# An attention and feed-forward kernel: phi, k and v on 128 partitions, and a front ordered by a list scheduler in the source

## The chip, the cores and the metric

The kernel runs on one core of a Trainium2 chip. TensorE (PE, with its weight loads PEld), VectorE (DVE), ScalarE (ACT), GpSimd (POOL) and SyncE (SP) each take their own instructions strictly in order; they wait for each other by semaphores. SP issues all loads of the front. The metric is the device time of one execution in microseconds (us), the median of several runs.

## What is computed

Four sequences b with eight heads of 576 positions each (head size 64, 32 memory slots). Attention goes through the memory; then come two feed-forward layers over all 2304 positions.

```python
a = softmax(phi, over slots)              # phi: (4, 8, 576, 32); the maximum is taken over positions
k_m = einsum('bhsm,bhsd->bhmd', a, k)     # v_m alike from v
attn = softmax(q @ k_m.T / 8)             # 32 columns
x = (attn @ v_m) as (2304, 512)
x = silu(x @ w_in) @ w_out                # 512 -> 2048 -> 512
out = ((x @ w_a) * (x @ w_b)) @ w_out2    # 512 -> 1536 -> 512
```

In the reference `phi - np.max(phi, axis=2)` takes the maximum over the 576 positions, for each slot. The weights come as 64-bit floats and are turned on the chip into two fp32r tiles each, a high (h) and a low part (l); each product is three fp32r matmuls (hh, hl, lh).

## The kernel before

The kernel has a front (attention of four sequences, and the first quarter f = 0 of the first layer for some units), the rest of the first layer, and the second layer. The front is what changes.

For each sequence b the front does the following. `weights(b)` (L443) takes the maximum of phi over positions on DVE (L450, tile mxa), across partitions by a PE transpose (mxt, L455) and a second maximum (mx, L459), brings it back to all partitions with a matmul (bc, L465), subtracts it (L472) and exponentiates (L475, tile ph). `memory(b)` (L493) multiplies ph by k and v (tile kvp, L506; one group of matmuls for each half hg of the heads, and one against a column of ones for the sums), normalises (rec, kvn), and makes kmT, the diagonal kbd (L548) and, over vt (L526), the value tiles vbd_hi and vbd_lo. `turn_q` (L535) transposes q into qT, `scores` (L542) makes sc by PE and x by a DVE transpose, and `softmax_part` (L566) makes x into at_hi and at_lo: maximum mxq, subtraction, Exp, sum smq, reciprocal, product, transpose xt, split. `vw_first` (L245) multiplies vbd by the weights w_in (tile mp, then m0h, m0l for b = 0, m1h, m1l for b = 1 and so on), so that a unit of the feed-forward layer is hp = m x at (`emit_h`, L279), silu, g, and yp = w_out x g (`emit_y`, L303).

phi, k and v lie on 96 partitions with 6 positions each (L416, L424), q on 128. The eight weight tiles of f = 0 go through `load_w` (L93): a 512 KB load into one of three buffers st, then e and t on ACT and DVE, with L124 or L122 the last to read st, and a split into h and l.

The source calls these pieces in an order written out by hand (L593 to L670); on each engine the framework's scheduler then orders the instructions. A load whose buffer is still read waits on SP, and all loads behind it wait too. The feed-forward units from the second half of b = 2 on follow in loops (L685). Weight tiles of f = 1 are loaded at fixed steps of the units (`due`, L331).

## Time and profile before

| | |
|---|---|
| median of 3 runs | 905.0 us (903.12 to 907.53) |
| profiled execution | 902.69 us |
| its span, first to last instruction | 900.9 us |
| PE busy in the span | 844.9 us (94%) |
| DVE, ACT, POOL busy | 536.2, 406.4, 162.5 us |
| mean granted TensorE clock | 0.962 of full speed |

In the page's forty slices PE is below 9 tenths in the first four (5, 3, 5, 8) and in the last one only (4), and the granted clock is below full in the first four and the last as well. A slice is 22.5 us long. So the time in which PE does not work at full speed lies in the first 90 us and in the last 20.

### The profile page before, as it was taken

What the parts mean: (1) busy time and instruction counts of PE and PEld (TensorE: products, weight loads), DVE (VectorE), ACT (ScalarE), POOL (GpSimd) and SP (SyncE); (2) the same over time, 40 slices, a digit from 0 to 9 for tenths busy, and PEclk for the clock granted to TensorE, in tenths of its full rate; (3) what the DMA queues carried; (4) which work ended last, traced back from release to release, by engine and by line L of the source; (5) the groups of instructions that cost most, each with busy time, mean ns of one, the idle gap of its engine ahead of it and who ended that gap; (6) DMA issues with size and microseconds to landing.
All of it is one profiled execution on the core that took longest, in us unless ns stands there. A gap on an engine that the chain in (4) does not pass through costs nothing.

```text
span 900.9 us, 14125 instructions
## 1 busy us (share of the span) xinstructions
PE 844.9 (94%) x5654; PEld 798.6 (89%) x5654; DVE 536.2 (60%) x980; ACT 406.4 (45%) x819; POOL 162.5 (18%) x160
## 2 busy tenths in 40 slices
PE   5358999999999999999999999999999999999994
PEld 4247989889999999999999999999999999999993
DVE  3699787887677676766665555545555453332221
ACT  2347676686565566655443333333333342222110
POOL 3454014422110211211221111101111110000000
PEclk7577999999999999999999999999999999999997
DMA  9988410356652554554764434424333330111101
GB/s 211 238 203 209 107 28 25 106 129 132 150 106 48 129 109 103 114 110 109 173 140 94 94 65 89 117 51 102 85 68 83 70 59 1 36 36 36 34 22 51
DMA packets 48858, 87.16 MB, mean 97 GB/s; under 512 B 3480, under 2 KB 24984, under 8 KB 48792
## 3 DMA queue, kind: packets, MB, share of 16 engines
q1 hardware_dynamic: 32664, 56.89, 23.7%
q0 software_dynamic: 16128, 29.37, 18.5%
q8 instruction: 44, 0.72, 0.3%
q14 instruction: 22, 0.18, 0.1%
HBM read 52.17 MB, written 4.72 MB: 63 GB/s over the span
## 4 chain that ended last, share of the span: by engine, by line
PE 83%; DVE 6%; DMA 5%; issue 2%; SPq 1%; ACT 1%; POOL 0%; DVEq 0%; POOLq 0%; ACTq 0%
PE ab L742 33%; PE yp L312 20%; PE op L763 17%; PE hp L288 9%; DMA st<-in_moe_w_in_dram 3%; PE mp L268 1%; PE mp L256 1%; PE sc L556 1%; DVE t L113 1%; DMA kv<-in_v_dram 1%; DMA wo_1l<-t_wo 1%; DVE qT L539 1%; SPq L427 1%; SPq L98 0%; DVE gl L300 0%
## 5 line engine op out<-in xcount | busy, mean ns | idle before, releaser
L747 DVE TENSOR_TENSOR asb<-ab,asb 128x384 f32<-128x384 f32 x72 | 40.1, 557 | 200.9 <-PE ab L742 200.9
L746 ACT ACTIVATE asb<-ab 128x384 f32<-128x384 f32 x72 | 35.4, 491 | 152.0 <-PE ab L742 145.4
L79 ACT ACTIVATE ph<-asb 128x384 fp32r<-128x384 f32 x72 | 37.5, 521 | 119.0 <-DVE asb L747 119.0
L298 ACT ACTIVATE g<-hp 128x288 f32<-128x288 f32 x128 | 52.2, 411 | 80.1 <-PE hp L288 71.9
L300 DVE TENSOR_TENSOR gl<-g,gh 128x288 fp32r<-128x288 f32 x128 | 62.2, 488 | 38.7 <-ACT gh L299 38.3
L187 POOL DMA_DIRECT2D t_w<-e_w x36 | 31.9, 885 | 145.8 <-DVE e_w L183 126.1
L318 DVE TENSOR_TENSOR y<-yp,y 128x288 f32<-128x288 f32 x104 | 47.3, 456 | 18.2 <-PE yp L312 17.5
L299 ACT ACTIVATE gh<-g 128x288 fp32r<-128x288 f32 x128 | 56.4, 444 | 3.6 <-PE yp L312 0.3
L75 DVE TENSOR_TENSOR pl<-asb,ph 128x384 fp32r<-128x384 f32 x72 | 39.9, 555 | 20.7 <-ACT ph L79 20.7
L79 ACT ACTIVATE yh<-y 128x768 fp32r<-128x768 f32 (+1 forms) x48 | 29.5, 676 | 25.5 <-PE ab L742 25.5
L312 PE MATMUL yp<-gh,wo_1l 128*128 128x288 f32 x128 | 37.8, 295 | 1.6 <-DMA wo_1l<-t_wo 1.6
L312 PE MATMUL yp<-gh,wo_0h 128*128 128x288 f32 x128 | 38.4, 300 | 0.1
L312 PE MATMUL yp<-gh,wo_2h 128*128 128x288 f32 x128 | 38.2, 298 | 0.0
L312 PE MATMUL yp<-gl,wo_3h 128*128 128x288 f32 x128 | 37.8, 297 | 0.0
L312 PE MATMUL yp<-gl,wo_2h 128*128 128x288 f32 x128 | 37.8, 295 | 0.0
L312 PE MATMUL yp<-gl,wo_0h 128*128 128x288 f32 x128 | 37.8, 295 | 0.0
L312 PE MATMUL yp<-gh,wo_2l 128*128 128x288 f32 x128 | 37.8, 295 | 0.0
L312 PE MATMUL yp<-gl,wo_1h 128*128 128x288 f32 x128 | 37.7, 296 | 0.0
L312 PE MATMUL yp<-gh,wo_3h 128*128 128x288 f32 x128 | 37.7, 295 | 0.0
L312 PE MATMUL yp<-gh,wo_1h 128*128 128x288 f32 x128 | 37.7, 294 | 0.0
L312 PE MATMUL yp<-gh,wo_0l 128*128 128x288 f32 x128 | 37.7, 294 | 0.0
L312 PE MATMUL yp<-gh,wo_3l 128*128 128x288 f32 x128 | 37.6, 294 | 0.0
(416 smaller groups left out, 2857.5 us busy)
## 6 DMA issues: line engine op xcount, KB each, us to landing
t_w<-e_w POOLq DMA_DIRECT2D x36, 256.0 KB, 4.7
st_wi<-in_moe_w_in_dram SPq DMA_DIRECT2D x12, 512.0 KB
st_wo<-in_moe_w_out_dram SPq DMA_DIRECT2D x12, 512.0 KB
st_w<-in_moe_w_a_dram SPq DMA_DIRECT2D x12, 512.0 KB
st_w<-in_moe_w_b_dram SPq DMA_DIRECT2D x12, 512.0 KB
st_w<-in_moe_w_out_dram SPq DMA_DIRECT2D x12, 512.0 KB
kv<-in_k_dram SPq DMA_DIRECT2D x8, 576.0 KB
kv<-in_v_dram SPq DMA_DIRECT2D x8, 576.0 KB
```

The lines of the kernel that those rows point to most:

```text
L75: eng_lo.tensor_tensor(out=lo, in0=src, in1=hi.bitcast(F32), op=ALU.subtract)
L79: nc.scalar.activation(out=out, in_=in_, func=AF.Copy)
L288: nc.tensor.matmul(hp, a[:, cs], x[b][:, kc, ts], start=(n == 0), stop=(n == 5))
L298: nc.scalar.activation(out=g32, in_=hp, func=AF.Silu)
L299: nc.scalar.activation(out=gh, in_=g32, func=AF.Copy)
L300: nc.vector.tensor_tensor(out=gl, in0=g32, in1=gh.bitcast(F32), op=ALU.subtract)
L312: nc.tensor.matmul(yp, a[:, os], x, start=(n == 0), stop=(n == 3 * len(cs) - 1))
L318: nc.vector.tensor_tensor(out=ys, in0=yp, in1=ys, op=ALU.add)
L742: nc.tensor.matmul(abp, a[:, ks], yy[:, kc], start=(n == 0), stop=(n == 11))
L746: nc.scalar.activation(out=asb, in_=ps[0], func=AF.Copy)
L747: nc.vector.tensor_tensor(out=asb, in0=ps[1], in1=asb, op=ALU.mult)
L763: nc.tensor.matmul(o_t[x], a[:, xs], w, start=(c == 0 and n == 0), stop=(c == 3 and n == 2))
```

## The change

phi, k and v are laid on 128 partitions: two heads side by side, 64 partitions with 9 positions each. The maximum of phi is a tree of four DVE instructions over tiles m4 and mxa instead of one reduction; its subtraction is on DVE for every b; the matmuls of kvp have 64 rows and there are 36 instead of 24 in a group. The softmax of the scores is done in two halves for every b. The front is no longer written in order: each piece is a generator that announces, before every instruction or group, its engine and a length in ns; `run` takes the one that can start first, by these lengths and by rank, and emits it. Each instruction is pinned (`Pinned`), so the framework keeps the source's order on every engine until `pinned[0] = False`, which stands behind the seventh unit. In a profile of it all pinned instructions bear one line, that of the helper.

```diff
     EPS = 1e-9
-    LATER = (nc.vector, nc.gpsimd, nc.gpsimd)
-    SPLIT = (0, 3)
-    SPLIT_W = (0,)
-    SPLIT_Q = ()
-    SUMS = (3,)
-    WARM = (16, 2, 0)
+    pinned = [True]
+
+    class Pinned:
+
+
+        def __init__(self, eng):
+            self.eng = eng
+
+        def __getattr__(self, name):
+            f = getattr(self.eng, name)
+
+            def call(*a, **k):
+                ins = f(*a, **k)
+                return tc.keep_in_program_order(ins) if pinned[0] else ins
+
+            return call
+
+    V, A, GP, T, Y = (Pinned(e) for e in (nc.vector, nc.scalar, nc.gpsimd, nc.tensor, nc.sync))
+    WARM = 16
...
-    P = 96
-    JP = S // P
+    JP = S // 64
...
-        ph = p_in.tile([P, H, JP, NM], F32, tag="ph", name="ph")
-        src = phi[b].rearrange("h (p c) m -> p h (c m)", p=P)
...
-        kv = p_in.tile([P, 2, 4, JP * D], F32, tag="kv", name="kv")
-        for i, s in enumerate((k, v)):
-            nc.sync.dma_start(
-                out=kv[:, i], in_=s[b, 4 * hg : 4 * hg + 4].rearrange("h (p c) d -> p h (c d)", p=P)
-            )
...
+    rings = dict(st=(3, []), e=(2, []), t=(2, []), ph=(2, []), kv=(2, []), qq=(3, []), qT=(1, []), x=(2, []),
+                 kvn=(1, []), mxq=(2, []), smq=(2, []), bank=(2, []), sc=(2, []), hp=(2, []), yp=(2, []), g=(8, []), m=(4, []), g32=(2, []))
...
+    def run(while_any):
+        while any(t[0] in while_any for t in tasks):
+            starts = [(start_of(t), t) for t in tasks]
+            starts = [(a, t) for a, t in starts if a is not None]
+            assert starts, [t[2] for t in tasks]
+            first, t = min(starts, key=lambda x: x[0])
+            eng = t[2][0]
+            rank, at, t = min(((t[0], a, t) for a, t in starts if t[2][0] == eng and a <= first + 200.0), key=lambda x: x[:2])
+            _, ns, _, done, takes, free, wait = t[2]
+            end = at + ns
...
+    def weights(b):
+
+        yield op("V", 1500, [f"phi{b}"])
...
-            nc.vector.tensor_reduce(
-                out=mxa, in_=e[:, hs].rearrange("p h c m -> p h m c"), op=ALU.max, axis=AX.X
-            )
...
+        m4 = p_s.tile([128, 4, 4, NM], F32, tag="m4", name="m4")
+        mxa = p_s.tile([128, 4, NM], F32, tag="mxa", bufs=2, name="mxa")
+        for o, x, y in (
+            (m4, e[:, :, 0:4], e[:, :, 4:8]), (m4[:, :, 0:2], m4[:, :, 0:2], m4[:, :, 2:4]),
+            (m4[:, :, 0], m4[:, :, 0], m4[:, :, 1]), (mxa, m4[:, :, 0], e[:, :, 8]),
+        ):
+            V.tensor_tensor(out=o, in0=x, in1=y, op=ALU.max)
...
+        yield op("V", 1350, free=[f"bc{b}"])
+        V.tensor_tensor(out=e, in0=e, in1=bc.unsqueeze(2).to_broadcast([128, 4, JP, NM]), op=ALU.subtract)
+        yield op("A", 1150, done=f"w{b}")
+        A.activation(out=e, in_=e, func=AF.Exp)
...
+            yield op("T", 3000, [f"w{b}", f"kv{b}{hg}"], take=("bank", f"kvp{b}") if hg == 0 else None,
+                     free=[f"kv{b}{hg}"] + [f"ph{b}"] * hg)
...
+                        o = slice(32 * h, 32 * h + 32)
+                        x, r = (h // 2 + b) % 2, slice(64 * (h % 2), 64 * (h % 2) + 64)
+                        T.matmul(
+                            kvp[o, hg, 2 * D :] if sums else kvp[o, hg, : 2 * D],
+                            e[r, 2 * hg + x, c],
+                            ones[r, :1] if sums else kv[r, :, x, c * D : c * D + D],
...
+            yield op("T", 1000, [f"kbd{b}"], done=f"sc{b}{hg}{hf}", take=("sc", f"sc{b}{hg}{hf}"), free=[f"qT{b}{hg}"] * hf)
...
+        sub, mul, low = HELP[b]
+        yield op("V" if sub is V else "G", 620 if sub is V else 1200, free=[f"mxq{b}{hg}"])
         sub.tensor_tensor(out=x, in0=x, in1=mx.unsqueeze(2).to_broadcast(full), op=ALU.subtract)
-        nc.scalar.activation(out=x, in_=x, func=AF.Exp, scale=scale)
-        sm = p_s.tile([128, n], F32, tag="smq", name="smq")
...
+        yield op("V", 700, free=[f"st_{name}"])
+        V.scalar_tensor_tensor(out=e, in0=low, scalar=2.0**-52, in1=e, op0=ALU.mult, op1=ALU.mult)
...
+            elif kind == "kv":
+                yield op("D", 3800, done=f"kv{b}{hg}", take=("kv", f"kv{b}{hg}"))
+                kv = st[b]["kv", hg] = p_in.tile([128, 2, 2, JP * D], F32, tag="kv", name="kv")
+                for i, s in enumerate((k, v)):
+                    src = s[b, 4 * hg : 4 * hg + 4].rearrange("(x r) (p c) d -> (r p) x (c d)", r=2, p=64)
+                    Y.dma_start(out=kv[:, i], in_=src)
...
-    load_phi(0)
+    LOADS = (
+        "phi00 wi00 kv00 q00 wi01 kv01 q01 wo00 phi10 phi20 wo01 wi02 wi03 kv10 q10 kv11 wo02 q11 kv20 q20 kv21 wo03 q21 phi30 kv30 q30 kv31 q31"
+    ).split()
+    HELP = ((GP, V, GP), (GP, GP, GP), (GP, V, GP), (GP, GP, GP))
     fill()
...
-    softmax(0, 0, nc.gpsimd, nc.gpsimd, nc.gpsimd)
-    load_kv(1, 1)
-    for kc in range(2):
-        vw_first(0, kc, (0,))
...
+    add(0, loads())
+    add(6, feed_forward())
+    for b in range(B):
+        add(2 + b, weights(b))
+        add(2 + b, memory(b))
+        add(2 + b, values(b))
+        for hg in range(2):
+            add(2 + b, scores(b, hg))
...
+    for c in range(4):
+        add((2, 2, 4, 4)[c], tile_of("wi", c, *((GP, GP), (GP, GP), (V, GP), (GP, V))[c]))
+        add((3, 2, 4, 3)[c], tile_of("wo", c, *((V, GP), (V, GP), (V, V), (V, GP))[c]))
+    run((0, 1, 2, 3, 4, 5))
+    run((1, 6))
+    pinned[0] = False
```

Three places in the order of instructions follow. In rows of before a line number tells the code; in rows of the change all have L69.

**SP, loads of the front.** st_ is the buffer of a weight tile, kv that of k or v for half of the heads of one sequence, qq that of q, ph of phi. In brackets stand the semaphores that a row waits for: DMAHW for an earlier load, the others for an engine. Before, from the fourth weight tile on (then k and v of b = 1, first half):

```order
L98 DMA st_386<-in_moe_w_out_dram 128x512 [waits DMAHW6_49,DVE_49,Activation_49]
L427 DMA kv<-in_k_dram 96x4x384 [waits DMAHW7_49,PE_49]
L427 DMA kv<-in_v_dram 96x4x384 [waits DMAHW0_49]
L98 DMA st_417<-in_moe_w_in_dram 128x2x256 [waits DMAHW1_49,Activation_49,Pool_49]
L421 DMA ph<-in_phi_dram 96x8x192 [waits DMAHW2_49,PE_49]
L427 DMA kv<-in_k_dram 96x4x384 [waits DMAHW3_49]
L427 DMA kv<-in_v_dram 96x4x384 [waits DMAHW4_49]
L98 DMA st_602<-in_moe_w_out_dram 128x512 [waits DMAHW5_49,Pool_49]
L98 DMA st_677<-in_moe_w_in_dram 128x2x256 [waits DMAHW6_49,DVE_49,Activation_49]
```

With the change, the rows from the second phi load's successor on; the second wi row here is the fourth tile of w_in, and k, v and q of b = 1 stand behind it:

```order
L69 DMA st_wo_367<-in_moe_w_out_dram 128x512 [waits DMAHW4_49,DVE_49]
L69 DMA st_wi_390<-in_moe_w_in_dram 128x2x256 [waits DMAHW5_49,DVE_49,Activation_49]
L69 DMA st_wi_502<-in_moe_w_in_dram 128x2x256 [waits DMAHW4_49,DMAHW6_49,DVE_49,Activation_49]
L69 DMA kv<-in_k_dram 128x2x576 [waits DMAHW7_49]
L69 DMA kv<-in_v_dram 128x2x576 [waits DMAHW0_49]
L69 DMA qq<-in_q_dram 64x1152 [waits DMAHW1_49]
L69 DMA qq<-in_q_dram 64x1152 [waits DMAHW2_49]
L69 DMA kv<-in_k_dram 128x2x576 [waits DMAHW3_49]
L69 DMA kv<-in_v_dram 128x2x576
```

Before, k and v of b = 1 stood behind one weight tile whose buffer was that of the first tile; they now stand behind three weight tiles, the last of which reuses the buffer of the tile that the next rows on DVE finish (st_wo_340).

**DVE, the tile of weights whose buffer is awaited.** Before, the load of the fourth w_in tile (st_677) waited for the buffer st_386, which the row with st_386 reads last:

```order
L113 SCALAR_TENSOR_TENSOR t_389<-e_388,t_389 128x512
L75 TENSOR_TENSOR vbd_lo_74<-vt,vbd_hi_72 64x2x32
L459 TENSOR_REDUCE mx<-mxt 128x2
L117 TENSOR_SCALAR e_388<-t_389 128x512
L75 TENSOR_TENSOR vbd_lo_74<-vt,vbd_hi_72 64x2x32
L124 SCALAR_TENSOR_TENSOR e_388<-st_386,e_388 128x512
L75 TENSOR_TENSOR vbd_lo_74<-vt,vbd_hi_72 64x2x32
L127 TENSOR_TENSOR t_389<-t_389,e_388 128x512
```

With the change the buffer st_wo_340 is read last by the row that has its name; the smq, x and xt above it are the softmax of b = 0, second half, and ph is the subtraction of b = 1:

```order
L69 TENSOR_REDUCE smq<-x 128x18
L69 TENSOR_SCALAR smq<-smq 128x18
L69 RECIPROCAL smq<-smq 128x18
L69 TENSOR_TENSOR x<-x,smq 128x576
L69 STREAM_TRANSPOSE xt<-x 128x576
L69 TENSOR_TENSOR ph<-ph,bc 128x1152
L69 TENSOR_SCALAR t_wo_476<-e_wo_382 128x512
L69 SCALAR_TENSOR_TENSOR t_wo_476<-e_wo_382,t_wo_476 128x512
L69 TENSOR_SCALAR e_wo_382<-t_wo_476 128x512
L69 SCALAR_TENSOR_TENSOR e_wo_382<-st_wo_340,e_wo_382 128x512
```

The last read of that buffer moved behind the whole softmax of b = 0.

**PE, scores of b = 1.** Before, the two groups of kvp for b = 1, then the scores sc of b = 1, first half, without anything of b = 2 between:

```order
L506 MATMUL kvp<-ones,ph 32x1 x24
L506 MATMUL kvp<-kv,ph 32x128 x24
L506 MATMUL kvp<-ones,ph 32x1 x24
L506 MATMUL kvp<-kv,ph 32x128 x24
L526 MATMUL vt<-ident,kvn 128x128 x2
L455 MATMUL mxt<-ident,mxa 128x96 x2
L288 MATMUL hp<-at_hi_64,m0h 128x288 x2
L556 MATMUL sc<-qT,kbd 128x288 x4
L465 MATMUL bc<-dg,ones 96x256
```

With the change, between the sc of one half of b = 1 stand the kvp groups of b = 2:

```order
L69 MATMUL vt<-ident,kvn 128x128 x2
L69 MATMUL sc<-qT,kbd 128x288 x2
L69 MATMUL kvp<-ones,ph 32x1 x36
L69 MATMUL kvp<-kv,ph 32x128 x36
L69 MATMUL sc<-qT,kbd 128x288 x2
L69 MATMUL mp<-wi_0h,vbd_hi_72 128x256
...
L69 MATMUL sc<-qT,kbd 128x288 x2
L69 MATMUL kvp<-ones,ph 32x1 x36
L69 MATMUL kvp<-kv,ph 32x128 x36
L69 MATMUL sc<-qT,kbd 128x288 x2
```

The kvp rows (ones, then kv) of b = 2 came between the two sc of each half of b = 1.

## Rows read from the trace of the kernel before

**Rows 1.** windows: busy us (instructions) per engine, granted clock, DMA share, GB/s

```profile
0.00:22.00 22.00, 12.38 (x186) 10.56 (x186) 7.21 (x7) 4.97 (x9) 7.92 (x14) 0.73 0.98 211
22.00:45.00 23.00, 8.93 (x66) 6.56 (x67) 14.90 (x29) 8.09 (x21) 9.62 (x7) 0.51 1.08 238
45.00:68.00 23.00, 11.75 (x216) 9.85 (x215) 21.77 (x34) 9.49 (x19) 12.34 (x8) 0.71 0.89 206
68.00:90.00 22.00, 19.51 (x94) 15.79 (x94) 21.81 (x31) 16.01 (x32) 10.69 (x6) 0.76 0.81 207
90.00:113.00 23.00, 21.97 (x322) 20.78 (x320) 16.58 (x31) 15.56 (x38) 1.00 (x1) 1.00 0.44 105
```

**Rows 2.** PE's timeline, four moments: start, length in us, [idle before <-releaser]

```profile
24.94 2.79 PE L506 MATMUL kvp<-kv,ph 96*32 96x128 f32 x48 [3.58 <-DMA kv<-in_v_dram]
...
67.51 0.85 PE L288 MATMUL hp<-at_hi,m0h 128*128 128x288 f32 x2 [0.93 <-ACT at_hi L79]
...
104.42 0.30 PE L288 MATMUL hp<-at_hi,m1h 128*128 128x288 f32 x1
...
160.46 0.30 PE L288 MATMUL hp<-at_hi,m3h 128*128 128x288 f32 x1
```

**Rows 3.** PE's timeline, lengths of five pieces

```profile
39.87 4.21 PE L556 MATMUL sc<-qT,kbd 128*128 128x288 f32 x8
...
121.81 2.83 PE L506 MATMUL kvp<-kv,ph 96*32 96x128 f32 x96
...
133.04 2.10 PE L556 MATMUL sc<-qT,kbd 128*128 128x288 f32 x8
...
158.06 0.30 PE L312 MATMUL yp<-gh,wo_0h 128*128 128x288 f32 x1
...
159.66 0.29 PE L288 MATMUL hp<-at_hi,m2h 128*128 128x288 f32 x1
```

**Rows 4.** DMA between 9 and 15 us: packets, MB, share of 16 engines

```profile
q1 hardware_dynamic: 898, 1.37, 108.4%
```

**Rows 5.** DMA between 24 and 30 us, the same

```profile
q1 hardware_dynamic: 600, 1.76, 105.0%
```

**Rows 6.** DVE's groups by form, first 160 us: busy us, mean ns

```profile
L539 DVE STREAM_TRANSPOSE qT<-qq 128x1152 f32<-128x1152 f32 x8 | 10.9, 1362 | 3.6 <-DMA qq<-in_q_dram 3.5
...
L113 DVE SCALAR_TENSOR_TENSOR t<-e,t 128x512 uint32<-128x512 uint32 x8 | 9.9, 1233 | 0.2
...
L450 DVE TENSOR_REDUCE mxa<-ph 96x256 f32<-96x1536 f32 x3 | 8.3, 2783 | 2.0 <-DMA ph<-in_phi_dram 2.0
...
L558 DVE STREAM_TRANSPOSE x<-sc 128x288 f32<-128x288 f32 x16 | 7.5, 471 | 1.1 <-PE sc L556 0.9
...
L117 DVE TENSOR_SCALAR e<-t 128x512 uint32<-128x512 uint32 x8 | 3.8, 470 | 0.1
...
L575 DVE TENSOR_REDUCE smq<-x 128x18 f32<-128x576 f32 x4 | 2.9, 733 | 1.5 <-ACT x L573 1.5
...
L472 DVE TENSOR_TENSOR ph<-ph,bc 96x1536 f32<-96x1536 f32 x1 | 1.7, 1741 | 0.0
```

**Rows 7.** DVE's timeline, one operation twice

```profile
23.07 0.69 DVE L113 SCALAR_TENSOR_TENSOR t<-e,t 128x512 uint32<-128x512 uint32 x1
...
64.39 1.66 DVE L113 SCALAR_TENSOR_TENSOR t<-e,t 128x512 uint32<-128x512 uint32 x1
```

**Rows 8.** POOL's timeline, at the second of them

```profile
64.04 1.47 POOL L122 TENSOR_TENSOR e<-st,e 128x512 f32<-128x512 f32 x1
```

**Rows 9.** ACT's groups by form, first 160 us

```profile
L298 ACT ACTIVATE g<-hp 128x288 f32<-128x288 f32 x23 | 9.1, 407 | 7.2 <-PE hp L288 4.3 <-DVE gl L300 2.7
...
L298 ACT ACT_TABLE_LOAD x6 | 7.7, 1283 | 0.8 <-DVE gl L300 0.7
...
L548 ACT ACTIVATE kbd<-kmT 32x128 f32<-32x128 f32 x16 | 4.9, 305 | 0.8 <-DVE kmT L523 0.6
...
L79 ACT ACTIVATE at_hi<-xt 128x576 fp32r<-128x576 f32 x4 | 2.7, 682 | 3.0 <-DVE xt L583 3.0
```

More of the change, by code (lines that the diff above doesn't have):

```diff
@@ new lines, in add, with start_of @@
+    def add(rank, gen, ready=0.0):
+        first = next(gen, None)
+        if first:
+            tasks.append([rank, gen, first, ready])
+    def start_of(t):
+        eng, _, after, _, takes, _, _ = t[2]
+        at = max(t[3], free_at[eng])
+        for x in after:
+            if x not in made:
+                return None
+            at = max(at, made[x])
+        for name, _ in takes:
+            bufs, keys = rings[name]
+            if len(keys) >= bufs:
+                x = "free", keys[-bufs]
+                if x not in made:
+                    return None
+                at = max(at, made[x])
+        return at
@@ new lines, in run @@
+    def run(while_any):
[8 more added lines that the diff above has]
+            end = at + ns
+            free_at[eng] = end
+            if eng == "D":
+                t[3] = end
+                end += 2000.0
+            else:
+                t[3] = end = end + wait
+            for name, x in takes:
+                rings[name][1].append(x)
+            if done is not None:
+                made[done] = end
+            for x in free:
+                if x[-1] == "*" and x not in made:
+                    made[x] = end
+                else:
+                    made["free", x.rstrip("*")] = end
+            t[2] = next(t[1], None)
+            if t[2] is None:
+                tasks.remove(t)
@@ L514, in memory @@
-        nc.vector.reciprocal(out=rec, in_=rec)
-        kvn = p_s.tile([128, 2, 3, D], F32, tag="kvn", name="kvn")
+        V.tensor_scalar_add(rec, kvp[:, :, 2 * D], EPS)
+        V.reciprocal(out=rec, in_=rec)
+        yield op("A", 650, [f"kmT{b - 1}"] if b else [], done=f"kvn{b}", take=("kvn", f"kvn{b}"), free=[f"kvp{b}"])
+        kvn = t["kvn"] = p_s.tile([128, 2, 3, D], F32, tag="kvn", name="kvn")
         for hg in range(2):
-            nc.scalar.activation(
+            A.activation(
@@ new lines, in scores @@
+                T.matmul(sc, kbd[:, hg, e], qT[:, e, ts], start=(e == 0), stop=(e == 1))
+            first = hg == hf == 0
+            yield op("V", 500, [f"x{b}"] * hg, done=f"x{b}" if first else None, take=("x", f"x{b}") if first else None,
+                     free=[f"sc{b}{hg}{hf}"])
+            if first:
+                t["x"] = p_s.tile([128, 2 * J, NM], F32, tag="x", bufs=2, name="x")
+            o = hg * S + hf * HALF
+            V.transpose(out=t["x"].rearrange("p j m -> p (j m)")[:, o : o + HALF], in_=sc)
@@ new lines, in scores @@
+        yield op("V", 800, [f"xt{b}"] * hg, done=f"xt{b}" if hg == 0 else None, take=("x", f"xt{b}") if hg == 0 else None,
+                 free=[f"x{b}*"])
+        if hg == 0:
+            t["xt"] = p_s.tile([128, 2, S], F32, tag="x", bufs=2, name="xt")
+        xt = t["xt"][:, hg]
+        V.transpose(out=xt, in_=x.rearrange("p j m -> p (j m)"))
+        yield op("A", 680)
+        copy(A, at_hi[b][:, hg], xt)
+        yield op("V" if low is V else "G", 620 if low is V else 1600, done=f"at{b}{hg}", free=[f"xt{b}*"])
```

551 lines of the change are left out of this document (257 added, 294 removed).

## Prediction

> **What bounds the kernel now.** I read the page's slices first, then the windows of the front, then PE's timeline, then who is late in it. From 90 us to the last 20 us PE works at nearly full share and full clock; only an earlier start of that state, or less work in it, can change the time. In the first 90 us PE is busy 12.4, 8.9, 11.8 and 19.5 us per window, at a granted clock of 0.73, 0.51, 0.71 and 0.76 [rows 1]. In the same rows the DMA share is 0.98, 1.08, 0.89, 0.81, and DVE is busy 21.8 of 23 and 21.8 of 22 us from 45 to 90. So two things bound the front: the loads first, then DVE. The first kvp group of the second half of b = 0 waits 3.58 us for v until 24.94; the first feed-forward matmul starts at 67.51, the first of b = 1 at 104.42, the first of b = 3 at 160.46 [rows 2].
>
> The profiled execution took 902.7 us, 2.3 below the median of the runs (905.0). I make the sum on the trace and carry its difference over to the median.
>
> **The yardstick.** After the first hp of b = 1 both kernels do much the same on PE, so I ask when the changed one starts that row (call it T) and what T would leave the end where it is. Twelve yp matmuls take 1.60 us from 158.06 to 159.66, so 0.133 each; eight records of sc, four matmuls, take 2.10 at full clock and 4.21 at half; 48 kv matmuls of kvp take 2.83 [rows 3]. Counted in the changed order, 240 hp and yp (32.0), 24 mp of 256 columns (2.9 by columns), 8 sc (4.2) and two kvp groups (36 kv at 2.83 / 48 each make 2.1, with the ones an estimated 2.7 a group, 5.4) lie from that row to the first hp of b = 3: 44.5 us. At that hp the changed order has done 24 yp less than before (3.2 us). Break-even is T = 160.5 - 3.2 - 44.5 = 112.8 us.
>
> **Loads.** DMA engines are full in the front, so a packet's cost is engine time over packets: 6 us x 16 x 1.084 / 898 = 116 ns at a mean of 1526 bytes [rows 4], and 168 ns at 2933 bytes [rows 5]. The line through both is 59 ns plus 0.037 ns a byte. On 128 partitions a phi load has 512 packets of 1152 bytes instead of 768 of 768, and a load of k or v 256 of 2304 instead of 384 of 1536. Divided by 16 and by a share of 1.07, phi falls from 3.95 to 3.05 us and a k and v pair from 5.2 to 4.3; q stays at 1.7, a w_in tile at 2.0, a w_out tile at 1.6. The loads up to the second k and v pair make 21.6 us before, and the wait for it ended at 24.94 [rows 2], so 3.3 us are first and last latency. With the change they make 17.5, and the wait ends at 20.8. The 36 kv matmuls at half clock take 1.5 x 2.79 = 4.2. So kvp of b = 0 ends at 25.0 (call it K). If the wider layout brought nothing per byte, K would be 28.8; at 300 GB/s throughout, near the fastest row [rows 5], about 22.8.
>
> **From K to the load that holds up SP.** The changed order puts the fourth w_in tile on SP ahead of all of k, v and q of b = 1, and it waits for the DVE row that reads st_wo_340 last; everything behind it on SP waits too. From K to that row DVE has 40 instructions. Priced by rows: a qT transpose 1.36; four x transposes at 0.47; four scalar-tensor-tensor instructions on weights and an add at 0.69; six tensor-scalars at 0.45; eight softmax instructions of 576 columns at 0.73; the subtraction from phi 1.74 x 1152 / 1536 = 1.3 [rows 6]; the max tree, by columns from 0.69 for 512 down, 1.5 (the reduction takes 2.78 [rows 6]); small ones (reciprocals, vbd_lo, m0l, kmT) about 3.7. Sum 21.7. To it come waits for sc, kmT and vbd_hi, one sc at half clock and two handovers, 3.5, and POOL's interference: the same operation takes 0.69 alone and 1.66 while POOL runs [rows 7, 8], and over the eight of L113 the mean is 1.23 [rows 6], so each POOL operation costs DVE some 0.5 us; six fall here, 3.0. So the load is issued at K + 28 = 53. From about K + 10 to then DMA has nothing to do, where before its share was 1.08 and 0.89 up to 68 [rows 1]. Bounds: no waits at all, K + 22; every POOL operation at 1 us and the clock at half, K + 32.
>
> **From there to the second kvp of b = 1.** Behind it come the tile (2.0), a kv pair (4.3), q (1.7) and a pair (4.3): 12.3 us plus 3.3 latency, then 4.2 of kv matmuls at half clock: 53 + 19.8 = 72.8 (call it E). PE has its feed-forward units of b = 0 to do meanwhile (48 hp and yp, 6.4 us), so T does not wait for them.
>
> **From E to T** the pinned order forms one zigzag. Reciprocal, kvn, kmT and kbd 3.7; one sc 1.05; the first kvp group of b = 2, which stands between the two sc of b = 1, 2.7; the other sc 1.05 (E + 8.5). Transposes of x and of the next q, 1.9 (10.4). Two sc and the second kvp group of b = 2 between them, with handovers 5.2 (15.6). On DVE sum, two weight instructions, transposes and maximum, 4.4 (20.0). Beside the POOL subtraction ACT has at_hi (0.68), two table loads (1.28), a silu pair (0.41 and much the same for gh), two copies like it and the exponential like at_hi, 5.6 from E + 19.4 on (25.0). ACT again: two copies, a table load, a silu pair, three short ones of kvn and kbd of b = 2 (four at 0.305), 5.4 (30.4) [rows 9]. Then PE does 8 sc, 24 mp, 24 yp and 6 hp ahead of the row, 11.1, with two waits for x of 0.4: E + 42.3. T = 115.1, or 2.3 late. DVE's own rows in this stretch sum to 32.8, so E + 33 is the lower end; with POOL's interference in full and half clock in gaps E + 49 is the upper one. After T, PE's twelve units take 12.0 us to the kvp of b = 3, but ACT ahead of that exponential has six silu pairs, three more table loads and two at_hi in a row: a wait of 2.4. The sum is 4.7 us late.
>
> **The other edits.** The tree saves 1.3 us of DVE for each b, the subtraction moved to DVE gives it back (1.3), and both are in the sums above; POOL loses its longest operations, and gains none that DVE waits for in K to E. Two warm-up matmuls and the diagonal (dg) go: PE and ACT are idle there, worth nothing. Six table loads more on ACT stand in the zigzag above. What follows the seventh unit is the same code, and I cost it at nothing; PE's short stalls there could grow or vanish, and both ends of the range have 2 us for them, which is a choice.
>
> **A rule on the 64-row matmuls.** Rows first: four sc matmuls of 288 columns take 2.10, so a 128-column one alone would take 0.23 and 48 of them 11.2 us; kvp takes 2.83 [rows 3], so four column groups run at once. I price the changed group by this fourfold overlap. The Trainium skill, TensorEngine Tiling (Array Packing), Gotcha 1: PSUM Pressure, says that different row tiles cannot access the same PSUM bank simultaneously. The changed groups alternate between upper and lower 64 rows and write one bank. If they then overlapped only in pairs, each group's price would double; no run here shows it yet.
>
> **Rivals.** (A) Faster: the zigzag runs at DVE's own pace, since a better packed DVE and quicker loads let each piece be ready when its turn comes. For it: DVE's rows from E to T sum to only 32.8, and PE's share in the front is half [rows 1]. K = 23, load issued at 47, E = 65, T = E + 37 = 102, 10.8 early less the 2.4: about 897. It decides when T falls below some 106. (B) No change: the late loads and the earlier first feed-forward row cancel, T between 107 and 112, 902 to 907 with the wait after. Against it: before, DMA's share does not fall below 0.98 up to 45 us [rows 1]. (C) Much slower: the two row halves exclude each other and the group doubles: K and E each 4.2 later, the two groups of b = 2 and the two of b = 3 2.7 each later: 19 more, 929. It shows from a kvp group of 4 us at full clock.
>
> **How the numbers follow.** The forecast is 905.0 + 4.7, so 910 us. Its own range: K from 22.5 to 28.8 and the two stretches at half their bounds, 904 to 918. Chances: forecast 0.43 (0.05 of it less than 4.5 us late), A 0.30, B 0.20, C 0.07. The range 896 to 922 takes in A's price and B and leaves out C and the outer tail of A, some 0.15 to 0.2. A measurement of this kernel tells about 0.5% (4.5 us) from no change. Faster by over that: A, 0.30; within: B and that part of the forecast, 0.25; slower: the rest and C, 0.45.
>
> **What would show it.** In the changed trace: the wait for v of the second half of b = 0 ends near 21; SP issues the fourth w_in tile near 53 and DMA idles ahead of it; the second kvp of b = 1 ends near 73; the first hp of b = 1 stands near 115; a kvp group at full clock takes 2.7 us. Wrong it would be if SP were free by 47, if DVE's share from 73 to 115 were over 0.9 (A), or if PE's idle time after 160 us fell or rose by more than 4 us.

## The result and the profile after

The changed kernel takes 909.73 us (908.48 to 913.59), the kernel before 903.19 (900.14 to 907.53) in the same series. The ratio is 1.0075, with a 95% interval of 1.0053 to 1.0097: slower by 5 to 9 us. Forecast were 910 us, 4.7 more than the 905.0 of the first three runs before; measured against 903.19 the loss is 6.5. The profiled execution took 909.73 us, its span is 908.0 (before 900.9); PE is busy 854.0 us of it (844.9), DVE 530.8, ACT 410.0, POOL 152.4.

The windows of the changed kernel over the front, cut as in [rows 1]:

```profile
0.00:22.00 22.00, 14.38 (x324) 13.07 (x325) 11.22 (x21) 6.54 (x12) 9.29 (x16) 0.84 0.82 289
22.00:45.00 23.00, 10.11 (x37) 7.07 (x36) 20.44 (x37) 7.33 (x19) 5.61 (x5) 0.76 0.38 135
45.00:68.00 23.00, 19.32 (x341) 17.05 (x341) 17.61 (x33) 13.64 (x25) 4.98 (x4) 0.65 0.73 216
68.00:90.00 22.00, 18.02 (x352) 15.57 (x353) 12.35 (x26) 9.21 (x21) 2.32 (x2) 0.92 0.77 252
90.00:113.00 23.00, 17.22 (x103) 15.33 (x103) 19.25 (x39) 16.60 (x34) 8.05 (x6) 0.93 0.34 108
```

DMA is no longer full over the first 45 us (share 0.82 and 0.38 instead of 0.98 and 1.08), and the first 22 us move 289 GB/s instead of 211. DVE is nearly full from 22 to 45 us (20.44 of 23), where before it was not (14.90), and not behind that: 12.35 of 22 us from 68 to 90. PE is busier than before in the first three rows and less in the last two (18.02 and 17.22 us; before 19.51 and 21.97).

PE's timeline of the changed kernel at the moments that answer to [rows 2]:

```profile
17.92 0.39 PE L69 MATMUL kvp<-ones,ph 64*32 64x1 f32 x27 [1.15 <-issue]
...
18.20 2.13 PE L69 MATMUL kvp<-kv,ph 64*32 64x128 f32 x70
...
56.98 4.04 PE L69 MATMUL kvp<-kv,ph 64*32 64x128 f32 x72
...
64.41 2.17 PE L69 MATMUL kvp<-kv,ph 64*32 64x128 f32 x72
...
71.94 2.16 PE L69 MATMUL kvp<-kv,ph 64*32 64x128 f32 x70
77.15 0.38 PE L69 MATMUL kvp<-kv,ph 64*32 64x128 f32 x2 [3.05 <-issue]
...
113.11 0.30 PE L69 MATMUL hp<-at_hi,m1h 128*128 128x288 f32 x1
...
128.98 0.87 PE L69 MATMUL kvp<-ones,ph 64*32 64x1 f32 x71 [2.16 <-ACT ph L69]
...
159.23 0.40 PE L69 MATMUL hp<-at_hi,m2h 128*128 128x288 f32 x1 [2.56 <-ACT g L69]
...
167.25 0.30 PE L69 MATMUL hp<-at_hi,m3h 128*128 128x288 f32 x1
```

The second kvp group of b = 0 ends at 20.3, that of b = 1 at 66.6; the first hp of b = 1 (T) stands at 113.11, where 112.8 was the break-even. Two stops of PE on ACT follow. Windows of 2 us around them, PE's columns alone (busy time and instructions, granted clock, DMA share, GB/s):

```profile
127.00:129.00 2.00, 0.02 (x3) 1.00 0.00 0
129.00:131.00 2.00, 2.00 (x100) 0.61 0.00 0
131.00:133.00 2.00, 2.00 (x48) 0.54 0.03 8
...
157.00:159.00 2.00, 0.00 (x0) 1.00 0.00 0
159.00:161.00 2.00, 1.77 (x10) 0.79 0.00 0
161.00:163.00 2.00, 2.00 (x11) 0.50 0.01 4
163.00:165.00 2.00, 2.00 (x15) 0.86 0.75 252
```

Behind each stop PE works at the lower clock level for a while. Busy time times what is missing of the clock makes 1.7 us behind the first stop and 1.65 behind the second, seven tenths of the stops' own 4.7. In the kernel before, no window of 4 us from 100 to 176 us is below full clock.

The account in the prediction's own terms: T is 0.3 us late. From T to the first hp of b = 3 it takes 54.1 us (113.11 to 167.25) where 44.5 us of work were counted; the stops of 2.16, 2.56 and two small ones of 1.0 together make 5.7, the lower clock 3.35, in all 53.6. So that row is 167.25 - 157.3 = 10 us behind its break-even. Later the changed kernel gets 2.3 us back: up to 240 us its waits of over 0.7 us behind that row are one of 0.8, where before has two of 1.6 (for m1l and for a weight tile). 10 - 2.3 = 7.7, and the spans differ by 7.1.

### The profile page after: what moved, and what is told of

Its sections match the earlier page's. It is cut to its first block, busy times and chain, and to the rows that moved or that the text cites. A ratio compares the mean times of both kernels' runs of the same rounds, so it can differ in the third digit from the quotient of the medians.

```text
span 908.0 us, 15049 instructions
## 1 busy us (share of the span) xinstructions
PE 854.0 (94%) x6116; PEld 808.3 (89%) x6116; DVE 530.8 (58%) x1003; ACT 410.0 (45%) x817; POOL 152.4 (17%) x161
## 3 DMA queue, kind: packets, MB, share of 16 engines
q1 hardware_dynamic: 29576, 56.89, 20.3%
## 4 chain that ended last, share of the span: by engine, by line
PE 81%; DVE 6%; ACT 5%; issue 3%; DMA 3%; POOL 1%; DVEq 0%; POOLq 0%; ACTq 0%
PE ab L69 32%; PE yp L69 17%; PE op L69 16%; PE hp L69 10%; PE kvp L69 3%; PE mp L69 2%; ACT L69 1%; DMA t_w<-e_w 1%; PE sc L69 1%; DVE t_wo L69 1%; DVE e_wo L69 1%; DVE x L69 1%; DMA wo_1l<-t_wo 1%; ACT g L69 1%; ACT gh L69 1%
## 5 line engine op out<-in xcount | busy, mean ns | idle before, releaser
L69 DVE TENSOR_TENSOR asb<-ab,asb 128x384 f32<-128x384 f32 x72 | 40.1, 557 | 202.4 <-PE ab L69 199.9
L69 ACT ACTIVATE asb<-ab 128x384 f32<-128x384 f32 x72 | 35.3, 491 | 151.7 <-PE ab L69 151.7
L69 ACT ACTIVATE ph<-asb 128x384 fp32r<-128x384 f32 x72 | 37.6, 522 | 119.8 <-DVE asb L69 119.7
L69 DVE TENSOR_TENSOR gl<-g,gh 128x288 fp32r<-128x288 f32 x128 | 62.0, 487 | 46.9 <-ACT gh L69 46.3
L69 ACT ACTIVATE g<-hp 128x288 f32<-128x288 f32 x128 | 52.2, 410 | 75.3 <-PE hp L69 71.9
L69 ACT ACTIVATE gh<-g 128x288 fp32r<-128x288 f32 x128 | 56.6, 444 | 3.9 <-PE yp L69 0.2
L69 DVE TENSOR_TENSOR y<-yp,y 128x288 f32<-128x288 f32 x104 | 47.3, 455 | 16.5 <-PE yp L69 16.2
L69 POOL DMA_DIRECT2D t_w<-e_w x36 | 31.8, 883 | 145.6 <-DVE e_w L69 127.3
L69 DVE TENSOR_TENSOR pl<-asb,ph 128x384 fp32r<-128x384 f32 x72 | 39.9, 555 | 19.5 <-ACT ph L69 19.5
L69 PE MATMUL yp<-gh,wo_0h 128*128 128x288 f32 x128 | 39.1, 306 | 4.2 <-ACT y L69 3.9
L69 ACT ACTIVATE yh<-y 128x768 fp32r<-128x768 f32 (+1 forms) x48 | 29.5, 676 | 26.0 <-PE ab L69 26.0
L69 PE MATMUL yp<-gh,wo_1l 128*128 128x288 f32 x128 | 38.0, 297 | 0.8 <-DMA wo_1l<-t_wo 0.8
L69 PE MATMUL yp<-gh,wo_2h 128*128 128x288 f32 x128 | 38.3, 299 | 0.0
L69 PE MATMUL yp<-gl,wo_1h 128*128 128x288 f32 x128 | 38.1, 298 | 0.0
L69 PE MATMUL yp<-gh,wo_0l 128*128 128x288 f32 x128 | 38.0, 297 | 0.0
L69 PE MATMUL yp<-gl,wo_0h 128*128 128x288 f32 x128 | 37.9, 296 | 0.0
L69 PE MATMUL yp<-gh,wo_1h 128*128 128x288 f32 x128 | 37.8, 296 | 0.0
L69 PE MATMUL yp<-gl,wo_2h 128*128 128x288 f32 x128 | 37.8, 295 | 0.0
L69 PE MATMUL yp<-gh,wo_2l 128*128 128x288 f32 x128 | 37.7, 295 | 0.0
L69 PE MATMUL yp<-gh,wo_3h 128*128 128x288 f32 x128 | 37.7, 295 | 0.0
L69 PE MATMUL yp<-gh,wo_3l 128*128 128x288 f32 x128 | 37.6, 294 | 0.0
L69 PE MATMUL yp<-gl,wo_3h 128*128 128x288 f32 x128 | 37.4, 295 | 0.0
```

Of the source, the lines that this page charges most:

```text
L69: ins = f(*a, **k)
```

## The experiments

| kernel | median, us | ratio to before (95%) | second kvp of b = 1 ends | T |
|---|---|---|---|---|
| changed kernel | 909.73 | 1.0075 (1.0053 to 1.0097) | 66.6 | 113.1 |
| e1_layout | 906.49 | 1.0039 (1.0018 to 1.0059) | 64.6 | 99.9 |
| e2_tables | 905.47 | 1.0027 (1.0008 to 1.0045) | 65.2 | 113.2 |
| e3_loads | 905.61 | 1.0031 (1.0008 to 1.0053) | 57.1 | 108.8 |
| e4_fill | 909.07 | 1.0060 (1.0037 to 1.0082) | 68.2 | 115.5 |
| e5_sums | 903.67 | 1.0004 (0.9984 to 1.0023) | 64.1 | 99.8 |
| e6_quiet | 905.94 | 1.0044 (1.0027 to 1.0061) | 68.1 | 111.1 |
| e7_list | 891.80 | 0.9883 (0.9863 to 0.9903) | 53.6 | 89.6 |
| e8_plan | 892.02 | 0.9880 (0.9860 to 0.9900) | 56.5 | 98.4 |
| e9_free | 910.98 | 1.0099 (1.0076 to 1.0123) | 76.0 | 102.0 |
| e10_list0 | 899.71 | 0.9978 (0.9961 to 0.9994) | 53.4 | 106.0 |
| e11_rows96 | 892.01 | 0.9882 (0.9862 to 0.9903) | 53.5 | 97.8 |
| e12_margin | 891.83 | 0.9880 (0.9858 to 0.9902) | 47.9 | 97.7 |

T compares only kernels with the same pieces ahead of it; between different orders it is a landmark, not a measure.

The question was which part of the change costs: the layout, the late T, or what happens behind T. The first four runs each take one of these.

**e1_layout.** The hand-written order of before with the new layout in its functions; the sums of b = 3 come from kvp, as in the changed kernel:

```diff
-        kv = p_in.tile([P, 2, 4, JP * D], F32, tag="kv", name="kv")
+        kv = p_in.tile([128, 2, 2, JP * D], F32, tag="kv", name="kv")
...
-            nc.vector.tensor_reduce(
-                out=mxa, in_=e[:, hs].rearrange("p h c m -> p h m c"), op=ALU.max, axis=AX.X
-            )
+            nc.vector.tensor_tensor(out=o, in0=x, in1=y, op=ALU.max)
...
+                            e[r, 2 * hg + x, c],
+                            ones[r, :1] if sums else kv[r, :, x, c * D : c * D + D],
```

> The kernel before in its hand-written order, with the new layout alone: phi, k and v on 128 partitions, the maximum by the tree, its subtraction on DVE, 36 matmuls of 64 rows in a kvp group; no list scheduler, no pins. Theory (the layout gains, the written order gives it away): loads of the front run at some 396 GB/s as in the changed kernel (9 to 15 us) instead of 228, the DMA-bound stretch up to 45 us shortens by some 6 us, DVE then bounds it, and the time is 895 to 901. Rival (the layout itself costs: 12 matmuls more in each group, subtraction on DVE instead of POOL while DVE is at 21.8 of 23 us): no gain, 902 to 910. The wait for v of the second half of b = 0, 24.94 before, ends near 19 under both.

Measured 906.49, in the rival's range: slower than before, by 0.2 to 0.6%. The trace shows why. T comes at 99.9, 4.5 us earlier than before. Then PE stops for long once. Its timeline and DVE's in e1_layout, at that place:

```profile
127.44 0.69 PE L492 MATMUL vt<-ident,kvn 128*128 128x128 f32 x2 [4.68 <-ACT kvn L487]
```

```profile
123.96 1.38 DVE L549 STREAM_TRANSPOSE xt<-x 128x1152 f32<-128x1152 f32 x1 [2.31 <-POOL x L544]
125.26 0.12 DVE L479 TENSOR_SCALAR rec<-kvp 128x2 f32<-128x2 f32 x1
```

kvp of b = 3 had ended at 119.2, but rec stands on DVE behind xt, which waits for POOL; ACT's kvn waits for rec, and PE's vt for that. Behind the stop 2.8 us go to the lower clock.

**e5_sums** takes that stop away: the sums of b = 3 come from a reduction and eight small matmuls, as before the change (L478, L489), so rec needs no kvp.

```diff
+        if b in SUMS:
+            es = p_s.tile([128, 4, NM], F32, tag="mxa", bufs=2, name="es")
+            nc.vector.tensor_reduce(out=es, in_=e.rearrange("p x c m -> p x m c"), op=ALU.add, axis=AX.X)
...
-            for sums in (1, 0):
+            for sums in (0,) if b in SUMS else (1, 0):
```

> The layout alone in the order written by hand, as in the run e1_layout, but the sums of b = 3 are made as before the change (a reduction es on DVE and 8 small matmuls in place of 72), so that rec of b = 3 no longer waits for kvp. In e1_layout the time stood 4.5 us ahead of before at the first hp of b = 1 (99.9 against 104.4) and lost it by one stop of 4.68 us at 127.4 (PE's vt waits for kvn, ACT for rec, and DVE has rec behind the transpose xt of b = 2) with half clock behind it, 2.8 us. Theory (layout gains, that stop eats it): the stop falls below 1 us, clock stays full, and the time is 897 to 901, below before. Rival (something else in the layout costs the 3.5 us): the stop goes or moves, the time stays 904 to 907.

Measured 903.67, a ratio of 1.0004, between the two cases. The stop is gone, and 2.8 us came back, but 897 to 901 was not reached: in the written order the layout gains nothing and loses nothing. T stays 4.6 us earlier than before, and the span is 902.7 against 900.9, so 6.4 us are lost behind T, in smaller pieces: PE's idle time from 100 to 240 us is 7.3 us where before it is 5.0, a lower clock around 204 us costs 1.5, and the kv parts of b = 3 take 4.1 us where before they take 2.83 [rows 3]. 1.3 us of it I can't assign.

**e2_tables.** The planner of the changed kernel counts the load of ACT's table; nothing else is different.

```diff
+            if table and table != loaded[0]:
+                loaded[0] = table
+                ns += 1280
             end = at + ns
```

> The changed kernel, whose planner counts 1280 ns on ACT for each change between exponential and silu; nothing else is changed, only the order that follows from it. Theory (the loss is two stops of PE behind T, 2.2 us before kvp of b = 3 and 2.6 at 156.7, each with some 3.7 us at half clock after it): the planner puts those pieces elsewhere, the stops shrink below 1 us each, granted clock stays 1.0 from 113 to 180, and 5 to 8 us come back: 902 to 905. Rival (the late start of b = 1 is the loss, T at 113): T does not come earlier by this, the time stays 908 to 912.

Measured 905.47, 4.3 us below the changed kernel, at the same T (113.2). The two stops shrink from 2.16 and 2.56 to 1.55 and 1.67, not below 1; PE's rows of e2_tables:

```profile
125.81 1.05 PE L69 MATMUL kvp<-ones,ph 64*32 64x1 f32 x72 [1.55 <-ACT ph L69]
...
158.67 0.40 PE L69 MATMUL hp<-at_hi,m2h 128*128 128x288 f32 x1 [1.67 <-ACT g L69]
```

The clock still falls after the first (0.50 from 126 to 128 us), not after the second (1.00 from 159 to 165). The direction was that of the theory; the time lies just above its 902 to 905, and below the rival's 908 to 912.

What ACT does ahead of the second stop in the changed kernel (its timeline):

```profile
154.16 0.44 ACT L69 ACTIVATE gh<-g 128x288 fp32r<-128x288 f32 x1
154.51 0.65 ACT L69 ACTIVATE e_wi<-st_wi 128x512 f32<-128x512 f32 x1
155.18 1.28 ACT L69 ACT_TABLE_LOAD   x1
156.47 0.68 ACT L69 ACTIVATE x<-x 128x576 f32<-128x576 f32 x1
157.06 0.39 ACT L69 ACTIVATE y<-yp 128x288 f32<-128x288 f32 x1
157.47 1.28 ACT L69 ACT_TABLE_LOAD   x1
158.77 0.41 ACT L69 ACTIVATE g<-hp 128x288 f32<-128x288 f32 x1
```

Between two silu pairs stand 4.2 us; the planner counted 1.8 for the three pieces between them and nothing for the two table loads, 2.6. PE's next hp waits for the second pair.

**e3_loads.** The list of loads alone; k, v and q of b = 1 come ahead of two weight tiles.

```diff
-        "... wo01 wi02 wi03 kv10 q10 kv11 wo02 ..."
+        "... wo01 kv10 q10 kv11 wi02 wi03 wo02 ..."
```

> The changed kernel with another list of loads: k, v and q of b = 1, first half, and k and v of the second half, stand ahead of the third and fourth w_in tile; the planner then orders the rest anew. Rival (SP's blocked queue makes the front late): second kvp of b = 1 ends by 55 instead of 66.6, T falls from 113.1 to 103 to 107, and the time to 900 to 904. Theory of the two stops behind T: T moves little, 109 to 113, since weights of b = 0, the softmax of b = 1 and ACT stand in the way too, the stops stay, 906 to 911.

Measured 905.61, 4.1 us below the changed kernel and just below the 906 to 911 of the second side. The execution that was profiled is the slowest of twelve, 909.98 us, so its marks can't be joined to that gain: in it the second kvp of b = 1 ends at 57.1 instead of 66.6 (expected was 55), T is 108.8, 4.3 us earlier, and the stops behind T stay (1.86 and 3.32). Both sides had a part of it: the blocked queue costs, and of the 9.5 us that kvp gained less than half is left at T, since PE then waits 4.5 us for kvn:

```profile
85.18 0.69 PE L69 MATMUL vt<-ident,kvn 128*128 128x128 f32 x2 [4.52 <-ACT kvn L69]
```

**e4_fill.** Ten matmuls more, into the bank that kvp of b = 3 then writes anew:

```diff
+                for _ in range(10 * (b == 3)):
+                    T.matmul(kvp[:, 0, : 2 * D], ident, ident, start=True, stop=True)
```

> The changed kernel with ten more 128x128 matmuls of ident on PE ahead of the first kvp of b = 3, where PE stops for 2.2 us; they write the kvp bank, whose values are then written anew. Theory (the stop costs its length and half clock after it): the stop is filled, kvp of b = 3 runs at full clock, 2.9 us a group instead of 4.5, and of the loss 1.5 to 2 us come back: 907.5 to 908.5. Rival (half clock there has another cause than the stop): the groups stay at 4.5 us and the time at 909.7 or a little above.

PE's windows of e4_fill at that place, the same columns as above:

```profile
127.00:129.00 2.00, 2.00 (x17) 1.00 0.01 4
129.00:131.00 2.00, 2.00 (x20) 1.00 0.00 0
131.00:133.00 2.00, 2.00 (x113) 1.00 0.00 0
133.00:135.00 2.00, 2.00 (x127) 1.00 0.03 8
```

With the stop filled the clock stays full, and the kv parts of the two groups take 2.2 and 2.5 us; in the changed kernel the first took 3.68. From T to the first hp of b = 3 it is 53.1 us instead of 54.1. The time, 909.07, cannot be told from 909.73, nor from the 907.5 to 908.5 of the theory. So the lower clock behind the stop is the stop's doing, and it costs 1 to 1.7 us there.

**e6_quiet** asks about the stop of 3.05 us inside kvp of b = 2, which no semaphore releases. SP is made to issue nothing more until kvp is through:

```diff
-        "... kv21 wo03 q21 phi30 kv30 q30 kv31 q31"
+        "... kv21 kv30 wo03 q21 phi30 q30 kv31 q31"
```

> The changed kernel with one thing moved in the list of loads: k and v of b = 3, first half, which wait for the buffer that kvp of b = 2 frees, stand ahead of the fourth w_out tile, the second half of q of b = 2 and phi of b = 3; so SP issues nothing more until kvp of b = 2 is through, and DMA has little to do from 71 to 77 us, where it had a share of 0.9 to 1.0. PE's order up to that place is the same. Question: the stop inside kvp of b = 2 (3.05 us, released by nothing that the profile shows). If PE's own instructions come over the same DMA engines and stand behind loads, the stop falls below 1 us, and T comes up to 3 us earlier, time 905 to 909. If it is anything else at this place (v of b = 2 late, a property of the 64-row matmuls), 3 us stay, 908 to 911.

PE's timeline of e6_quiet at the same two instructions:

```profile
73.53 2.16 PE L69 MATMUL kvp<-kv,ph 64*32 64x128 f32 x70
76.04 0.38 PE L69 MATMUL kvp<-kv,ph 64*32 64x128 f32 x2 [0.35 <-issue]
```

The stop stands at the same matmul and lasts 0.35 us. DMA's queues in the 2 us in which the stop begins (packets, MB, share of 16 engines), first the changed kernel from 74 to 76, then e6_quiet from 74 to 76:

```profile
q1 hardware_dynamic: 398, 0.74, 97.8%
q8 instruction: 1, 0.02, 2.9%
```

```profile
q1 hardware_dynamic: 4, 0.01, 0.9%
```

In the changed kernel a packet of the queue named instruction travels among full queues just then; in e6_quiet one had come between 72 and 74 us, and DMA is empty. The times of these packets fit: one starts at 74.8 in the changed kernel, 2.4 us before PE goes on at 77.15, and at 73.6 in e6_quiet, 2.4 us before 76.04; in e2_tables, e4_fill, e7_list, e8_plan, e10_list0 and e12_margin a stop of 2.6 to 3.8 us ends in the same way, 2.3 to 2.8 us behind the start of such a packet. T is 111.1, and the time 905.94, as the first case said. Part of the 3.8 us is the rest of the plan, which changed behind that place.

**e7_list.** The lengths of e2_tables and another list, searched for the earliest end in the planner's own reckoning.

```diff
+            if table and table != loaded[0]:
+                ns += 1280
...
-        "phi00 wi00 kv00 q00 wi01 kv01 q01 wo00 phi10 phi20 wo01 wi02 wi03 kv10 q10 kv11 wo02 q11 kv20 q20 kv21 wo03 q21 phi30 kv30 q30 kv31 q31"
+        "phi00 wi00 phi10 wo00 wi01 q00 kv00 kv01 wo01 wi03 phi20 q01 kv11 kv10 wi02 wo02 q10 q11 wo03 q21 q31 q20 kv21 kv20 kv30 phi30 q30 kv31"
```

> The changed kernel with the planner that counts 1280 ns for each change of function on ACT, and another list of loads, searched for the earliest end in the planner's own reckoning (132.7 against 147.8 us for the old list, same lengths; first hp of b = 1 planned at 82.6 against 103.2). Nothing else changes. If a late T and ACT's stops are the loss: T falls to 92 to 102 in the trace, and the time to 895 to 902, below before. If lengths that the planner does not know (half clock, POOL slowing DVE, packets) decide, the gain of 15 us in the plan is not found: 903 to 909.

Measured 891.80, 11 us below before and 18 below the changed kernel, below what was expected. PE's windows of e7_list, the same columns:

```profile
0.00:22.00 22.00, 11.79 (x254) 0.77 0.81 288
22.00:45.00 23.00, 16.64 (x238) 0.70 0.85 271
45.00:68.00 23.00, 18.61 (x252) 0.85 0.37 119
68.00:90.00 22.00, 20.16 (x391) 1.00 0.73 233
90.00:113.00 23.00, 22.23 (x157) 1.00 0.23 90
113.00:135.00 22.00, 20.98 (x394) 1.00 0.09 26
135.00:158.00 23.00, 21.48 (x153) 1.00 0.14 47
```

PE's idle time in these 158 us is 26.1 us; the changed kernel has 38.5 in the same windows (3.2 from 113 to 135 and 1.3 from 135 to 158, the rest in the rows shown above). That makes 12.4 us of the 18.8 by which the spans differ (908.0 and 889.2). Some 5 are the clock by the same reckoning as above (1.00 from 68 us on, where the changed kernel has 0.92 to 0.93 up to 135; 0.85 against 0.65 from 45 to 68), and the second stop behind 158 us does not come. DMA works from 22 to 45 us at 0.85 instead of 0.38: loads that are wanted later are under way then. The stop of e6_quiet's question is not gone; it stands inside a kvp group of b = 1:

```profile
47.25 1.71 PE L69 MATMUL kvp<-kv,ph 64*32 64x128 f32 x27 [3.19 <-issue]
```

**e10_list0.** That list with the planner's first lengths.

> The list of loads of e7_list with the planner as it was changed first, without lengths for the change of function on ACT (planned end 138.0, first hp of b = 1 planned at 94.5). If the list is nearly all of what e7_list gained (17.9 us), since the lengths alone gave 4.2 in e2_tables: 893 to 897. If list and lengths work only together, because the wrong lengths put exponentials between silu pairs again: 898 to 905, with stops of PE on ACT behind T.

Measured 899.71, as the second case said. The stop of 2.56 us on ACT g is back, and one of 3.92 on POOL:

```profile
72.31 0.58 PE L69 MATMUL mp<-wi_2l,vbd_hi 128*128 128x256 f32 x1 [3.92 <-POOL wi_2l L69]
...
149.86 0.40 PE L69 MATMUL hp<-at_hi,m2h 128*128 128x288 f32 x1 [2.56 <-ACT g L69]
```

So the list gives 10 us and the lengths 8 more with it; with the old list they gave 4.3. It is not the number of table loads: e10_list0 has 12 of them, e7_list 16, the changed kernel 18.

**e8_plan and e12_margin** let the search choose ranks and helpers too, with lengths of loads nearer to the trace, and in e12_margin, whose ranks are shown, with margins for slow DVE pieces and the lower clock.

```diff
-                yield op("D", 3800, done=f"kv{b}{hg}", take=("kv", f"kv{b}{hg}"))
+                yield op("D", 3100, done=f"kv{b}{hg}", take=("kv", f"kv{b}{hg}"))
...
-        add((2, 2, 4, 4)[c], tile_of("wi", c, *((GP, GP), (GP, GP), (V, GP), (GP, V))[c]))
+        add((5, 1, 2, 4)[c], tile_of("wi", c, *((GP, GP), (GP, GP), (GP, GP), (GP, GP))[c]))
```

> As e7_list, with loads planned at lengths nearer to the trace (phi 1600, k and v 3100, q 1800, a tile 1500 ns), and ranks of the weight tiles and the choice between DVE and POOL for some operations searched as well; planned end 129.8, first hp of b = 1 planned at 83.6. If a late T and ACT's stops are the loss: T at 92 to 100, time 893 to 901. If the planner's missing lengths decide: 903 to 909.

> As e8_plan, with the list, ranks and helpers searched for a planned end that also holds when DVE's pieces last 15% longer and kvp before 60 us 60% longer (half clock). Planned end 129.1, first hp of b = 1 at 84.5. If the plan's slips (10 to 15 us between planned and traced T) come from these two, the plan keeps more of its gain: 884 to 891. If they come from elsewhere (instruction fetch, packets): about as e7_list, 890 to 894.

Measured 892.02 and 891.83: no better than e7_list, though their planned ends are 3 and 4 us earlier, each by its own lengths. e8_plan lies just below its first case, e12_margin in its second: the margins bring nothing that can be measured, so by that expectation the plan's slips come from elsewhere.

**e9_free** takes the pins away.

```diff
-    pinned = [True]
+    pinned = [False]
```

> The changed kernel without its pins: the planner writes the source's order as before, and the framework may move instructions on each engine. If the pinned zigzag is the loss (PE held behind a piece that isn't ready): PE fills its stops at 127, 157 and 74 us with feed-forward matmuls, and the time is 900 to 906. If the list of loads and what follows from it decide, pins or not: 906 to 914.

Measured 910.98, the second case: with this list the pins are not the loss. T is 102.0, 11 us earlier, and the time is no better. PE still stops, 3.98 us at 119.9 and 3.65 at 160.3.

**e11_rows96.** Last, the old layout under the scheduler of e7_list, with a list searched for it in the same manner and two buffers for q instead of three:

```diff
-        for o, x, y in (
+        V.tensor_reduce(out=mxa, in_=e.rearrange("p h c m -> p h m c"), op=ALU.max, axis=AX.X)
...
-                kv = st[b]["kv", hg] = p_in.tile([128, 2, 2, JP * D], F32, tag="kv", name="kv")
+                kv = st[b]["kv", hg] = p_in.tile([P, 2, 4, JP * D], F32, tag="kv", name="kv")
...
-                yield op("D", 3800, done=f"kv{b}{hg}", take=("kv", f"kv{b}{hg}"))
+                yield op("D", 5200, done=f"kv{b}{hg}", take=("kv", f"kv{b}{hg}"))
```

> The list scheduler with the old layout: phi, k and v on 96 partitions, maximum by one reduction, 24 matmuls in a kvp group, two buffers for q instead of three for space; the planner counts 1280 ns for a change of function on ACT and the old lengths (k and v 5200 ns), and the list of loads is searched for it as for e7_list (planned end 137.5, against 132.7 there). If the scheduler with a good list is the gain and the layout adds little, as in e5_sums (no change in the old order): 892 to 898. If the layout is what lets the scheduler gain (loads at half the rate leave DMA the bound up to 45 us): 899 to 906.

Measured 892.01, the same as e7_list. Two lines of e11_rows96's windows, all engines:

```profile
22.00:45.00 23.00, 11.09 (x75) 8.04 (x76) 20.52 (x33) 7.97 (x21) 5.46 (x5) 0.55 1.09 264
...
68.00:90.00 22.00, 21.23 (x308) 19.21 (x307) 20.38 (x36) 18.35 (x33) 8.07 (x7) 1.00 0.91 214
```

DMA is full again up to 45 us, and PE has less done by then (11.09 us against 16.64). But with 24 matmuls in a group its work is less too: busy 838.9 us in all against 847.3, so that it idles 50.4 us of the span where e7_list idles 41.9. The two cancel.

## Why the prediction was right, and where not

The total was right (910 forecast, 909.73 measured, slower by more than 0.5%), and T nearly (115.1 and 113.1). Its parts were not; errors of both signs met. That the total came out to 0.3 us is luck: the loss was forecast at 4.7 and measured at 6.5, and before was taken at 905.0, which turned out at 903.19. Of the three signs of being wrong one came true, that of SP; DVE's share from 73 to 115 was 0.69, and PE's idle time after 160 us fell by 2.4, where 4 was the bound.

**Loads, K.** The wait for v was to end at 20.8 and K to be 25.0; kvp ran from 18.2 to 20.3. No row shows a wait for v: PE's last stop ahead of it is the 1.15 us of "issue" at 17.92. Of the 4.7 us, 2.6 are the earlier start and 2.1 the clock, full where half was priced. The step that failed is the line of packet costs from [rows 4, 5]. By it a packet of 2434 bytes takes 149 ns. DMA between 9 and 15 us in the changed kernel (packets, MB, share):

```profile
q1 hardware_dynamic: 978, 2.38, 104.6%
```

6 us x 16 x 1.046 / 978 is 103 ns, less than the 116 of the smaller packets of [rows 4]. The line drew the two layouts' difference as one of bytes alone, through two means over packets of several sizes. The packets' records in the two traces show more: between 9 and 15 us one of 1536 bytes (k and v on 96 partitions) took 125 ns before, and one of 2304 bytes (k and v on 128) 99 ns with the change. What makes the narrower layout's packets slower is open. One bound does not follow either: the changed list at the old layout's prices sums to 20.05, which makes 27.6 of K, not 28.8. In four of five later profiles of kernels with the same beginning (e3_loads, e4_fill, e6_quiet, e9_free; not e2_tables) the clock is low in that group and the group takes 3.4 to 4.0 us, so K is about 22 there: that much differs between executions.

**The load that holds up SP.** It was put at 53, behind the row that reads st_wo_340, and wrong "if SP were free by 47". SP's timeline and DVE's rows:

```profile
21.46 18.40 SPq L69 DMA_DIRECT2D st_wi<-in_moe_w_in_dram  x2
```

```profile
37.54 1.87 DVE L69 SCALAR_TENSOR_TENSOR e_wo<-st_wo,e_wo 128x512 f32<-128x512 uint32 x1
...
47.27 0.69 DVE L69 SCALAR_TENSOR_TENSOR e_wo<-st_wo,e_wo 128x512 f32<-128x512 uint32 x1
```

SP was free at 39.9, so the step was wrong by its own sign. I had taken the wrong buffer, there and in the section on the change: the fourth w_in tile takes that of st_wo_367, whose last reader ends at 39.4; the row at 47.27, which I had priced, frees the buffer for the next w_out tile, issued at 47.99. The price itself was nearly met, K + 27.7 for K + 28. The idle DMA ahead of it was there (share 0.01 from 27 to 39 us), for 12 us instead of 18.

**E and T.** E came at 66.6 instead of 72.8. From E to T were 42.3 forecast and 46.5 measured, within the bounds of 33 and 49. It holds the 3.05 us of the stop inside kvp of b = 2, which no step had, and a wait of 3.93 for ACT's y at 94. That this zigzag, not DVE's pace, sets the stretch was right (DVE share 0.56 and 0.84 in two rows), and rival A with T = 102 was refuted for this list. Rival B (T from 107 to 112, 902 to 907) lay just below both marks. e7_list shows what A was after: with another list and the table loads counted the same pieces do run at a pace that brings 891.8.

**Behind T.** The wait of 2.4 for ACT's exponential was 2.16, at the place named. The mechanism, ACT held by table loads, was right, and the second such stop was missed (2.56 at 156.7), as was the clock behind both (3.35). "What follows the seventh unit is the same code, and I cost it at nothing" failed in both directions: PE stops for the last silu pair of the seventh unit, and later waits shrank by 2.3.

**Rival C** is refuted: the kv part of a group takes 2.17 at full clock and 4.04 at half, with 0.77 for the ones 2.9 in all, against 2.7 forecast and 5.4 if halves of 64 rows excluded each other. The rule of the Trainium skill on row tiles and one PSUM bank (TensorEngine Tiling (Array Packing), Gotcha 1: PSUM Pressure) does not show here as a loss of overlap.

What the runs add on the cause: the layout by itself is worth nothing that could be measured, in two orders (e5_sums, and e11_rows96 against e7_list); the pins cost nothing with that list (e9_free); the order made from that list of loads and lengths without table loads loses 3 us to the hand-written order with the same layout and sums (909.7 and 906.5, e1_layout), 6 to it with the sums of b = 3 made as before (903.7, e5_sums), and 18 to the same planner with a better list and those lengths. The pins with the better list, the softmax in halves for every b and the warm-up matmuls left out have no run of their own.
